# Two transposes of the first eight tiles, from the DMA queue to the matrix engine

## The chip, the core and the metric

The kernel runs on one core of a Trainium2 chip. The core has a matrix engine (TensorE, PE in the profile, with PEld for its weight loads), a vector engine (VectorE, DVE), a scalar engine (ScalarE, ACT), GpSimd (POOL) and SyncE (SP), which here issues DMAs alone. Data lies in SBUF, 128 partitions wide; matmuls write to PSUM, eight banks of 512 float32 per partition. The metric is the device time of one execution in microseconds (us); lower is better.

## What is computed

Eight batches of 576 rows, eight heads of 64. Keys and values are first averaged over groups of eight rows, so that each row of q meets 72 keys. Softmax, product with the averaged values, heads put side by side (512 columns), then a normalised row, a feed-forward block 512 to 2048 to 512, and the residual:

```python
    k_p = k.reshape(B, H, Sp, pool, D).mean(axis=3)
    v_p = v.reshape(B, H, Sp, pool, D).mean(axis=3)
    scores = scale * np.matmul(q, k_p.transpose(0, 1, 3, 2))
    scores = scores - np.max(scores, axis=-1, keepdims=True)
    attn = np.exp(scores)
    attn = attn / (np.sum(attn, axis=-1, keepdims=True) + 1e-09)
    return np.matmul(attn, v_p).astype(np.float32)
...
    xn = (x - mu) / np.sqrt(var + 1e-06) * g_ln
    ch = np.maximum(xn @ w_ch1, 0.0) @ w_ch2
    return (x + ch).astype(np.float32)
```

Inputs and output are float32. Nearly every product is made of float16 parts: a number x is split into hi = float16(x) and lo = float16(x - hi), and hi*hi + hi*lo + lo*hi are summed in PSUM.

## The kernel before

The 4608 rows are 36 tiles of 128 rows, t = 0 to 35; four tiles are a chunk, c = 0 to 8. Three stages work on a tile:

- **A.t** (`stage_a`: `scores`, `probs`). Four float32 matmuls (L279; each shows as two instructions in the profile) make the scores of 8 heads x 72 keys in PSUM. VectorE takes the row maximum (L288) and subtracts it into the SBUF tile `e` (L289). ScalarE makes the exponential (L298) and two float16 copies (L299, L302) into `phl`; GpSimd puts the low parts beside them (L306, L309); one DMA transpose on SP's queue (L316) brings the lot to `pt`, keys on partitions.
- **B.t** (`values`). Sixteen matmuls (L335, L336; 65 columns: 64 of v and one for the sum) multiply `pt` with the split values `va` and `vb`. VectorE and ScalarE normalise (L339 to L352), VectorE makes mean and variance (L356, L357) and the inverse root by three Newton steps of two one-column instructions each (L371, L374), and the normalised row `z` (L378). ScalarE makes its high part (L382), GpSimd the low part (L383), and a second DMA transpose (L387) writes both to `zT` of the chunk.
- **FFN.** `ffn_in` (L406) makes 128 rows of the hidden layer for up to 512 columns of `zT` in 12 matmuls; ScalarE and VectorE evict the high and low part (L414, L415). `ffn_out` (L435) multiplies back for one tile and one half of the hidden layer in 24 matmuls of 512 columns; VectorE adds the result to the residual (L445).

Beside the tiles the kernel prepares what they use: **C.m.b** converts a 1 MB block of weights that comes as 64-bit words into float32 (L163 and L175 on ScalarE, L166 and L167 on VectorE; 16 blocks), **S.m.b** splits one into hi (ScalarE, L138) and lo (VectorE, L139), once **M** has found the scale over half a matrix (a small matmul, L126, spreads a maximum over partitions). `load_k`, `pool_k`, `load_v`, `pool_v` load and average keys and values (**HK**, **HV** for half a batch; GpSimd, in batch 0 VectorE too), and `split_v` splits the values and copies them with four small DMAs to the second half of `va` and `vb`.

The order of recording is a table of tokens, `START`, for chunks 0 and 1 (A.0 to A.11, B.0 to B.11, all weights; **I.c.q** is a quarter of the hidden layer in `ffn_in`, in chunk 0 by half chunks, **O.c.h** a half of it in `ffn_out`), and a loop for chunks 2 to 8. The framework's scheduler then settles each engine's own order; engines run strictly in that order and wait for each other by semaphores. PSUM holds two banks for scores (`ps_s`), two for values (`ps_x`), and four single banks (`ps_f`).

Of the kernel before, what the change touches and what calls it, by code (L numbers as in the profile page):

```python
# [48 lines left out]
HK.1.1 R.2.1 S.1.0 HV.1.0 B.2 B.3 HV.1.1 A.4 S.1.1 S.1.2 A.5 S.1.3 C.2.1 I.0.0.0 R.1.4 B.4 C.1.4
I.0.1.0 B.5 R.2.2 A.6 R.2.3 B.6 I.0.1.1 C.2.3 A.7 C.2.2 C.2.0 M2.0 R.2.4 S.2.0 R.1.5 S.2.1 S.2.2  # L50
R.1.6 R.1.7 S.2.3 B.7 I.0.0.1 O.0.0 C.1.5 I.1.1 C.1.6 I.1.0 C.1.7 M1.1 S.1.4 S.1.5 O.1.0 R.2.5 S.1.6
R.2.6 S.1.7 C.2.4 I.0.2 A.8 R.2.7 C.2.5 C.2.7 HK.2.0 HV.2.0 C.2.6 HK.2.1 B.8 M2.1 S.2.4 A.9 HV.2.1
A.10 B.9 I.0.3 S.2.5 S.2.6 HK.3.0 HK.3.1 I.1.2 B.10 S.2.7 O.0.1 I.1.3 A.11 HV.3.0 B.11 HV.3.1 O.1.1
# [6 lines left out]
def attn_ffn_kernel(ctx: ExitStack, tc: tile.TileContext, qT, kT, v, g, w1, w2, out):  # L60
# [235 lines left out]
    def probs(t):  # L296
        e, ph = E.pop(t), phl[t % 2]
        nc.scalar.activation(out=e, in_=e, func=AF.Exp, scale=EXP_SCALE)  # L298
        nc.scalar.copy(  # L299
# [18 lines left out]
    def values(t):  # L318
# [11 lines left out]
        ps = ps_x.tile([P, 2, 512], F32, name="ps_x")  # L330
        px = ps[:, :, : H // 2 * (D + 1)].rearrange("p a (h d) -> p a h d", d=D + 1)
        for r, b in segs:
            for h in range(H):
# [1 line left out]
                nc.tensor.matmul(o, lhsT=pt[:, h, r], rhs=VA[b][:, h, :], start=True, stop=False)  # L335
# [46 lines left out]
        nc.scalar.copy(out=zhl[:, 0, :], in_=z)  # L382
        nc.gpsimd.tensor_tensor(out=zhl[:, 1, :], in0=z, in1=zhl[:, 0, :], op=ALU.subtract)  # L383
# [182 lines left out]
```

## Time and profile before

| | |
|---|---|
| runs | 903.48, 904.53, 905.30 us; median 904.53 |
| profiled execution | 902.32 us, of which 900.3 us from its first to its last instruction (the span) |
| busy in the span | PE 828.9, PEld 419.2, DVE 436.1, ACT 263.9, POOL 262.3 us |
| DMA traffic | 84.80 MB in 137288 packets |

The page cuts the span into 40 slices of 22.5 us and gives each engine's busy share in tenths. The rows of windows that follow give busy us (and instructions) of PE, PEld, DVE, ACT and POOL in a stretch, the granted clock of PE, the busy share of the 16 DMA engines and GB/s. Rows of a timeline give start, duration, engine, line, operation, tiles and shape, and in brackets the idle time before and what ended it. Rows of groups give busy us, mean ns of one, and the idle time in front of them.

### The profile page before, as it was taken

What the parts mean: (1) busy time and instruction counts of PE and PEld (TensorE: products, weight loads), DVE (VectorE), ACT (ScalarE), POOL (GpSimd) and SP (SyncE); (2) the same over time, 40 slices, a digit from 0 to 9 for tenths busy, and PEclk for the clock granted to TensorE, in tenths of its full rate; (3) what the DMA queues carried; (4) which work ended last, traced back from release to release, by engine and by line L of the source; (5) the groups of instructions that cost most, each with busy time, mean ns of one, the idle gap of its engine ahead of it and who ended that gap; (6) DMA issues with size and microseconds to landing.
All of it is one profiled execution on the core that took longest, in us unless ns stands there. A gap on an engine that the chain in (4) does not pass through costs nothing.

```text
span 900.3 us, 11947 instructions
## 1 busy us (share of the span) xinstructions
PE 828.9 (92%) x4524; PEld 419.2 (47%) x4524; DVE 436.1 (48%) x1022; ACT 263.9 (29%) x513; POOL 262.3 (29%) x414
## 2 busy tenths in 40 slices
PE   2247975999999999999999999999999999999998
PEld 2236733444444444454445544544544454444443
DVE  7797994335462543256335533653354335432121
ACT  3766743314131221223123312331232123211020
POOL 6796596104233150056002710230011002100000
PEclk9999996999999999999999999999999999999999
DMA  8999975102252313253223432332223121310001
GB/s 316 268 246 279 283 224 136 27 0 65 77 127 75 62 57 72 59 135 88 66 59 83 116 71 59 86 70 55 59 59 80 39 59 36 70 38 22 1 1 47
DMA packets 137288, 84.80 MB, mean 94 GB/s; under 512 B 116112, under 2 KB 117264, under 8 KB 135184
## 3 DMA queue, kind: packets, MB, share of 16 engines
q1 hardware_dynamic: 135696, 82.86, 35.2%
q10 hardware_dynamic: 1536, 1.20, 0.5%
q8 instruction: 35, 0.57, 0.3%
q14 instruction: 21, 0.17, 0.1%
HBM read 45.09 MB, written 9.44 MB: 61 GB/s over the span
## 4 chain that ended last, share of the span: by engine, by line
PE 84%; DMA 7%; DVE 5%; ACT 1%; issue 1%; SPq 1%; POOL 1%; ACTq 0%
PE ps_f L406 40%; PE ps_f L435 39%; PE ps_s L279 2%; DMA raw<-in_w_dram 2%; DMA vr<-in_v_dram 2%; PE ps_x L335 1%; DVE y L374 1%; PE ps_x L336 1%; DVE w L167 1%; DMA pt<-phl 1%; DMA ring<-in_w_dram 1%; DMA raw<-in_v_dram 1%; DMA zT<-hl 1%; DVE a L371 0%; DVE raw L166 0%
## 5 line engine op out<-in xcount | busy, mean ns | idle before, releaser
L406 PE MATMUL ps_f<-zT,w 128*128 128x512 f16 (+1 forms) x1824 | 385.2, 370 | 4.3 <-DVE ring L415 2.9
L435 PE MATMUL ps_f<-w,ring 128*128 128x512 f16 x1728 | 380.9, 380 | 6.2 <-DVE w L139 5.9
L406 PEld LDWEIGHTS <-w 128*128 128x128 f16 x1824 | 177.8, 98 | 194.4 <-issue 8.9
L435 PEld LDWEIGHTS <-ring 128*128 128x128 f16 x1728 | 168.6, 98 | 206.7 <-issue 8.5
L415 DVE SCALAR_TENSOR_TENSOR ring<-ps_f,ring 128x512 f16<-128x512 f32 (+1 forms) x152 | 99.6, 659 | 139.6 <-ACT ring L414 139.3
L414 ACT ACTIVATE ring<-ps_f 128x512 f16<-128x512 f32 (+1 forms) x152 | 86.9, 574 | 264.9 <-PE ps_f L406 240.8
L445 DVE SCALAR_TENSOR_TENSOR x<-ps_f,c_out,x 128x512 f32<-128x512 f32 x72 | 53.9, 748 | 190.6 <-PE ps_f L435 190.5
L306 POOL TENSOR_TENSOR phl<-e,phl 128x512 f16<-128x512 f32 x36 | 43.8, 1218 | 261.1 <-ACT phl L299 248.5
L279 PE MATMUL ps_s<-kblk,q 128*128 128x144 f32 (+1 forms) x320 | 56.3, 345 | 43.7 <-issue 23.2
L383 POOL TENSOR_TENSOR hl<-z,hl 128x512 f16<-128x512 f32 x36 | 42.1, 1169 | 126.1 <-ACT hl L382 122.1
L298 ACT ACTIVATE e<-e 128x576 f32<-128x576 f32 x36 | 24.6, 683 | 168.9 <-DVE e L289 162.9
L279 PEld LDWEIGHTS ps_s<-kblk,q 128*128 128x128 f32 (+1 forms) x320 | 49.0, 219 | 51.5 <-issue 33.8
L352 ACT ACTIVATE x<-ps_x,rs 128x64 f32<-128x64 f32 x144 | 33.3, 314 | 81.1 <-DVE x L345 46.0
L229 POOL TENSOR_TENSOR vr<-vr 72x256 f32<-72x256 f32 x56 | 44.8, 805 | 22.3 <-DMA vr<-in_v_dram 22.0
L299 ACT CAST phl<-e 128x1024 f16<-128x1024 f32 x36 | 37.5, 1042 | 5.3 <-DMA pt<-phl 4.8
L382 ACT CAST hl<-z 128x512 f16<-128x512 f32 x36 | 22.2, 618 | 55.0 <-DVE z L378 45.5
L356 DVE BATCH_NORM_STATS2 st<-x 128x6 f32<-128x512 f32 x36 | 24.9, 691 | 23.4 <-ACT x L352 23.3
L231 POOL TENSOR_TENSOR vp<-vr 72x64 f32<-72x64 f32 x56 | 18.5, 345 | 60.5 <-DVE vb L139 60.3
L219 POOL TENSOR_TENSOR kblk<-kr 64x72 f32<-64x72 f32 x58 | 23.8, 411 | 32.1 <-PE ps_s L279 29.2
L215 POOL TENSOR_TENSOR kr<-kr 128x288 f32<-128x288 f32 x29 | 24.1, 833 | 27.1 <-DMA kr<-in_kT_dram 26.8
L335 PE MATMUL ps_x<-va,pt 128*128 128x65 f16 (+1 forms) x320 | 27.4, 200 | 4.9 <-ACT x L352 3.5
L288 DVE TENSOR_REDUCE mx<-ps_s 128x8 f32<-128x576 f32 x36 | 27.0, 751 | 9.3 <-PE ps_s L279 9.2
(81 smaller groups left out, 488.8 us busy)
## 6 DMA issues: line engine op xcount, KB each, us to landing
raw<-in_w_dram SPq DMA_DIRECT2D x12, 1024.0 KB
q<-in_qT_dram SPq DMA_DIRECT2D x36, 256.0 KB
out_dram<-x SPq DMA_DIRECT2D x36, 256.0 KB
kr<-in_kT_dram SPq DMA_DIRECT2D x30, 288.0 KB
vr<-in_v_dram SPq DMA_DIRECT2D x56, 144.0 KB
ring<-in_w_dram SPq DMA_DIRECT2D x4, 1024.0 KB
raw<-in_v_dram SPq DMA_DIRECT2D x8, 144.0 KB
va<-vh ACTq DMA_DIRECT2D x16, 65.0 KB
```

What stands on the lines that cost most here:

```text
L229: eng.tensor_add(out=vr[:, 0:4, :], in0=vr[:, 0:4, :], in1=vr[:, 4:8, :])
L279: nc.tensor.matmul(ps[r, p // 2, p % 2 * 2 * KV : (p % 2 + 1) * 2 * KV], lhsT=q[:, p, r], rhs=kblk[b % NKB][:, p, :], start=True, stop=True,)
L299: nc.scalar.copy(out=ph[:, :, :, 0:KA], in_=e[:, :, 0:KA].unsqueeze(1).broadcast_to([P, 2, H, KA]))
L306: nc.gpsimd.tensor_tensor(out=ph[:, 0, :, KA:P], in0=e[:, :, 0:KA], in1=ph[:, 0, :, 0:KA], op=ALU.subtract)
L335: nc.tensor.matmul(o, lhsT=pt[:, h, r], rhs=VA[b][:, h, :], start=True, stop=False)
L352: nc.scalar.activation(out=xh[:, 4 + i, :], in_=px[:, 1, i, 0:D], func=AF.Copy, scale=rs[:, 4 + i : 5 + i])
L383: nc.gpsimd.tensor_tensor(out=zhl[:, 1, :], in0=z, in1=zhl[:, 0, :], op=ALU.subtract)
L406: nc.tensor.matmul(ps, lhsT=w[:, part, fs], rhs=zT[:, kz, cols], start=(n == 0), stop=(n == 3 * NKT - 1),)
L414: nc.scalar.activation(out=h[:, 0, i, cols], in_=ps, func=AF.Relu)
L415: nc.vector.scalar_tensor_tensor(out=h[:, 1, i, cols], in0=ps, scalar=0.0, in1=h[:, 0, i, cols], op0=ALU.max, op1=ALU.subtract,)
L435: nc.tensor.matmul(ps, lhsT=h[:, part, i, cols], rhs=w[:, wp, j], start=(n == 0), stop=(n == 3 * NFT // 2 - 1),)
L445: nc.vector.scalar_tensor_tensor(out=x, in0=ps, scalar=c_out[:, half : half + 1], in1=x, op0=ALU.mult, op1=ALU.add)
```

## The change

For tiles t < 8 (`XT`) both DMA transposes go. In `probs` the float32 `e` is transposed by eight matrix-engine transposes against a float32 identity (new line L306) into two PSUM banks, 72 partitions x 1024. ScalarE copies this to float16 as the high part (L311), VectorE subtracts that from PSUM for the low part (L312). In `values` such a tile takes 24 matmuls in place of 16 (hi with `vh`, hi with `vb`, lo with `vh`). In `ffn_in`'s input, `z` goes through four transposes (L409), a ScalarE copy (L410) and a VectorE subtraction (L411). The float16 copies, GpSimd subtractions and SP transposes of these tiles fall away; tiles 8 to 35 keep them. The four small DMAs of `split_v` fall away for batch 0. Scores, transposed probabilities and values share one PSUM pool `ps_2` of two two-bank buffers; the pool of small scalars has two buffers in place of three. `START` has the same tokens in another order.

```diff
--- before.py
+++ after.py
@@ -38,6 +38,7 @@
 NQ = 4
 FPQ = NFT // NQ
 NKB = 2
+XT = 8
 A_AT, B_AT = (0, 6, 10, 14), (5, 9, 13, 19)
 
 EXP_SCALE = 1.0 / (POOL * D**0.5)
@@ -45,12 +46,12 @@
 Z_EXP, W1_EXP = -2, 7
 OUT_EXP = -14 - Z_EXP - W1_EXP
 START = """
-LD K0 R.1.0 V0 A.0 R.1.1 B.0 A.1 R.1.2 C.1.2 C.1.0 B.1 A.2 R.1.3 C.1.1 HK.1.0 C.1.3 A.3 R.2.0 M1.0
...
+LD K0 V0 R.1.0 A.0 R.1.1 B.0 R.1.2 A.1 B.1 R.1.3 C.1.3 C.1.0 C.1.2 A.2 A.3 R.2.0 C.1.1 HK.1.0 HK.1.1
...
 """
 RSQRT_MAGIC = float(0x5F3759DF - 0x00400000)
 Z_VAR = 2.0 ** (-1 - 2 * Z_EXP)
@@ -67,9 +68,8 @@
     ring = ctx.enter_context(tc.tile_pool(name="ring", bufs=4))
     rawp = ctx.enter_context(tc.tile_pool(name="rawp", bufs=2))
     xres = ctx.enter_context(tc.tile_pool(name="xres", bufs=8))
-    small = ctx.enter_context(tc.tile_pool(name="small", bufs=3))
-    ps_s = ctx.enter_context(tc.tile_pool(name="ps_s", bufs=1, space=PSUM))
-    ps_x = ctx.enter_context(tc.tile_pool(name="ps_x", bufs=1, space=PSUM))
+    small = ctx.enter_context(tc.tile_pool(name="small", bufs=2))
+    ps_2 = ctx.enter_context(tc.tile_pool(name="ps_2", bufs=2, space=PSUM))
     ps_f = ctx.enter_context(tc.tile_pool(name="ps_f", bufs=4, space=PSUM))
 
 
@@ -82,6 +82,8 @@
     wm = {m: const.tile([P, WB], F32, name=f"wm{m}") for m in (1, 2)}
     ident = const.tile([P, P], BF16, name="ident")
     make_identity(nc, ident)
+    ident32 = const.tile([P, P], F32, name="ident32")
+    nc.scalar.copy(out=ident32, in_=ident)
     kblk = [const.tile([P, NPAIR, 2 * KV], F32, name=f"kblk{i}") for i in range(NKB)]
     phl = [const.tile([P, 2, H, P], F16, name=f"phl{i}") for i in range(2)]
     for t in kblk:
@@ -203,6 +205,7 @@
 
 
     kraw = {}
+    VH = {}
     VA, VB, CV, vp, vmax, vraw = {}, {}, {}, {}, {}, {}
 
     def load_k(b, p, kr=None, queue=nc.sync):
@@ -239,7 +242,8 @@
 
     def split_v(b):
         e, s = vmax.pop(b), scalar_tile("sv")
-        vh = wk1.tile([KV, H, D + 1], F16, name="vh")
+        VH[b] = vh = wk2.tile([KV, H, D + 1], F16, name="vh")
+        dup = (b + 1) * S > XT * P
         VA[b] = wk2.tile([P, H, D + 1], F16, name="va")
         VB[b] = wk2.tile([KB, H, D + 1], F16, name="vb")
         nc.vector.memset(vh[:, :, D : D + 1], 1.0)
@@ -248,7 +252,7 @@
         CV[b] = wk3.tile([P, 1], F32, name="cv")
         nc.vector.tensor_scalar_mul(out=CV[b], in0=e, scalar1=2.0**-16)
         split(vp.pop(b), s[:KV], vh[:, :, 0:D], VB[b][:KV, :, 0:D])
-        for i in range(2):
+        for i in range(2 if dup else 0):
             nc.scalar.dma_start(out=VA[b][i * KA : (i + 1) * KA], in_=vh[:KA])
             nc.scalar.dma_start(out=VB[b][KV + i * KR : KV + (i + 1) * KR], in_=vh[KA:])
 
@@ -273,7 +277,7 @@
         E[t] = e = wk1.tile([P, H, KV], F32, name="e")
         q = q_sb.pop(t)
         mx = scalar_tile("mx", H)
-        ps = ps_s.tile([P, 2, 512], F32, name="ps_s")
+        ps = ps_2.tile([P, 2, 512], F32, name="ps_2")
         for p in range(NPAIR):
             for r, b in segments(t):
                 nc.tensor.matmul(
@@ -296,6 +300,17 @@
     def probs(t):
         e, ph = E.pop(t), phl[t % 2]
         nc.scalar.activation(out=e, in_=e, func=AF.Exp, scale=EXP_SCALE)
+        if t < XT:
+            ps = ps_2.tile([P, 2, 512], F32, name="ps_2")
+            for h in range(H):
+                nc.tensor.transpose(
+                    out=ps[:KV, h // 4, h % 4 * P : (h % 4 + 1) * P], in_=e[:, h], identity=ident32
+                )
+            PT[t] = pt = wk2.tile([P, 2 * H, P], F16, name="pt")
+            hi, src = pt[:KV, 0:H], ps[:KV].rearrange("p a (h n) -> p (a h) n", n=P)
+            nc.scalar.copy(out=hi, in_=src)
+            nc.vector.tensor_tensor(out=pt[:KV, H:], in0=src, in1=hi, op=ALU.subtract)
+            return
         nc.scalar.copy(
             out=ph[:, :, :, 0:KA], in_=e[:, :, 0:KA].unsqueeze(1).broadcast_to([P, 2, H, KA])
         )
@@ -327,11 +342,17 @@
         pt = PT.pop(t)
         sm, rs = scalar_tile("sm", H), scalar_tile("rs", H)
         X[t] = x = xres.tile([P, DM], F32, name="x")
-        ps = ps_x.tile([P, 2, 512], F32, name="ps_x")
+        ps = ps_2.tile([P, 2, 512], F32, name="ps_2")
         px = ps[:, :, : H // 2 * (D + 1)].rearrange("p a (h d) -> p a h d", d=D + 1)
         for r, b in segs:
             for h in range(H):
                 o = px[r, h // 4, h % 4]
+                if t < XT:
+                    vl = VB[b][:KV, h, :]
+                    hi, lo = pt[:KV, h, r], pt[:KV, H + h, r]
+                    for n, (w, m) in enumerate(((hi, VH[b][:, h, :]), (hi, vl), (lo, VH[b][:, h, :]))):
+                        nc.tensor.matmul(o, lhsT=w, rhs=m, start=(n == 0), stop=(n == 2))
+                    continue
                 nc.tensor.matmul(o, lhsT=pt[:, h, r], rhs=VA[b][:, h, :], start=True, stop=False)
                 nc.tensor.matmul(
                     o, lhsT=pt[:KB, H + h, r], rhs=VB[b][:, h, :], start=False, stop=True
@@ -378,15 +399,21 @@
         nc.vector.tensor_scalar(
             out=z, in0=x, scalar1=mv[:, 0:1], scalar2=y, op0=ALU.subtract, op1=ALU.mult
         )
+        c, tt = divmod(t, TPC)
+        if tt == 0:
+            zTs[c] = wk2.tile([P, 2 * NKT, CH], F16, name="zT")
+        zT = zTs[c][:, :, tt * P : (tt + 1) * P]
+        if t < XT:
+            ps = ps_f.tile([P, CH], F32, name="ps_f").rearrange("p (k n) -> p k n", n=P)
+            for k in range(NKT):
+                nc.tensor.transpose(out=ps[:, k], in_=z[:, k * P : (k + 1) * P], identity=ident32)
+            nc.scalar.copy(out=zT[:, 0:NKT], in_=ps)
+            nc.vector.tensor_tensor(out=zT[:, NKT:], in0=ps, in1=zT[:, 0:NKT], op=ALU.subtract)
+            return
         zhl = wk2.tile([P, 2, DM], F16, name="hl")
         nc.scalar.copy(out=zhl[:, 0, :], in_=z)
         nc.gpsimd.tensor_tensor(out=zhl[:, 1, :], in0=z, in1=zhl[:, 0, :], op=ALU.subtract)
-        c, tt = divmod(t, TPC)
-        if tt == 0:
-            zTs[c] = wk2.tile([P, 2 * NKT, CH], F16, name="zT")
-        nc.sync.dma_start_transpose(
-            out=zTs[c][:, :, tt * P : (tt + 1) * P], in_=zhl.rearrange("p a d -> p (a d)")
-        )
+        nc.sync.dma_start_transpose(out=zT, in_=zhl.rearrange("p a d -> p (a d)"))
 
 
     hT = {}
```

What the scheduler makes of it is shown at three places. Line numbers of the changed kernel are up to 27 higher: L141 there is L139 before, L433 is L406, L442 is L415, L462 is L435, L472 is L445, L283 is L279, L292 and L293 are L288 and L289, L354 to L357 are the value matmuls.

**VectorE at the first split of a block of the second weight matrix (w2), which `O.0.0` needs.** Before, it stands among the work on tiles 5, 6 and 9 (`st` and `mv` are tile 5's, `sm` and `rs` tile 6's, `e` tile 9's):

```order
L356 BN_STATS st<-x 128x6
L289 TENSOR_TENSOR e<-ps_s,mx 128x576
L339 TENSOR_SCALAR sm<-ps_x 128x8
L167 SCALAR_TENSOR_TENSOR w_88<-w_88,raw 128x1024
L415 SCALAR_TENSOR_TENSOR ring<-ps_f,ring 128x256 x2
L357 BN_AGGR mv_878<-st 128x2
L342 RECIPROCAL rs<-sm 128x8
L139 SCALAR_TENSOR_TENSOR w_89<-w_89,ws 128x1024
```

Now it stands behind the sum, scale and normalisation of tile 7 (`sm`, `rs`, `x` are that tile's):

```order
L200 TENSOR_TENSOR ws<-f_88,s_1164 128x1
L360 TENSOR_SCALAR sm<-ps_1404 128x8
L249 MEMSET vh 72x8
L442 SCALAR_TENSOR_TENSOR ring<-ps_f,ring 128x256
L363 RECIPROCAL rs<-sm 128x8
L364 TENSOR_SCALAR rs<-rs,cv 128x8
L366 TENSOR_TENSOR x<-ps_1404,rs 128x256
L141 SCALAR_TENSOR_TENSOR w_86<-w_86,ws 128x1024
```

The rest of tiles 5 and 6 up to `z`, the sums of tile 7 and the last three of the 16 conversions have moved in front of the split; the scores of tiles 8 and 9 have moved behind it.

**The matrix engine where `O.0.0` begins (`ffn_out` of chunk 0, first half).** Before, the values of tile 6 follow its first matmul:

```order
L406 MATMUL ps_f<-zT,w_88 128x256
L435 LDWEIGHTS ring
L435 MATMUL ps_f<-w_89,ring 128x512
L335 LDWEIGHTS pt
L335 MATMUL ps_x<-va,pt 128x65
```

Now the values of tile 7 stand ahead of it, and three of the four score matmuls of tile 8 (`ps_1728`) follow its first matmul:

```order
L433 MATMUL ps_f<-zT,w_85 128x256
L462 LDWEIGHTS ring
L462 MATMUL ps_f<-w_86,ring 128x512
L283 MATMUL ps_1728<-kblk_102,q 128x144 x3
L462 LDWEIGHTS ring
```

Before, the values of tiles 6 and 7 and the scores of tile 10 lay among the matmuls of `O.0.0`; now those values stand ahead of it and those scores behind it.

**The matrix engine where `I.1.1` begins (first `ffn_in` of chunk 1, 512 columns).** Before, three of tile 11's score matmuls and those of tiles 12 and 13 stand in front of it, these with 64 rows for each of two batches (`kblk_102` and `kblk_103`):

```order
L279 MATMUL ps_s<-kblk_103,q 64x144
L279 MATMUL ps_s<-kblk_102,q 64x144
L279 MATMUL ps_s<-kblk_103,q 64x144
L406 LDWEIGHTS w_88
L406 MATMUL ps_f<-zT,w_88 128x512
```

Now `O.0.0` ends, then come the transposes of tile 7's `z`, the values of tile 8 and the scores of tile 9:

```order
L462 LDWEIGHTS ring
L462 MATMUL ps_f<-w_86,ring 128x512
L409 MATMUL ps_f<-ident_99,z 128x128 x4
L356 LDWEIGHTS pt
L356 MATMUL ps_1847<-va,pt 128x65
```

```order
L357 MATMUL ps_1847<-vb,pt 128x65
L283 MATMUL ps_1902<-kblk_101,q 128x144 x4
L433 LDWEIGHTS w_85
L433 MATMUL ps_f<-zT,w_85 128x512
```

In front of `I.1.1` there stood the scores of 14 tiles before, and now those of 10.

More of the change, by code (lines that the diff above doesn't have):

```diff
@@ L47 @@
 START = """
-LD K0 R.1.0 V0 A.0 R.1.1 B.0 A.1 R.1.2 C.1.2 C.1.0 B.1 A.2 R.1.3 C.1.1 HK.1.0 C.1.3 A.3 R.2.0 M1.0
[L49 to L53, printed above, removed]
+LD K0 V0 R.1.0 A.0 R.1.1 B.0 R.1.2 A.1 B.1 R.1.3 C.1.3 C.1.0 C.1.2 A.2 A.3 R.2.0 C.1.1 HK.1.0 HK.1.1
+HV.1.0 M1.0 R.2.1 S.1.0 B.2 S.1.1 B.3 HV.1.1 A.4 S.1.2 A.5 C.2.1 S.1.3 I.0.0.0 R.1.4 C.2.0 B.4 A.6
+R.2.2 I.0.1.0 B.5 I.0.1.1 C.2.2 B.6 R.2.3 C.2.3 C.1.4 M2.0 R.2.4 S.2.0 R.1.5 R.1.6 S.2.1 A.7 I.0.0.1
+C.1.6 R.1.7 S.2.2 S.2.3 C.1.5 O.0.0 HK.2.0 B.7 I.1.1 I.1.0 C.1.7 M1.1 S.1.4 O.1.0 R.2.5 S.1.5 S.1.6
+R.2.6 S.1.7 R.2.7 C.2.4 A.8 I.0.2 C.2.5 HK.2.1 C.2.6 HV.2.0 B.8 C.2.7 A.9 M2.1 S.2.4 S.2.5 HV.2.1
+A.10 S.2.6 I.0.3 B.9 HK.3.0 I.1.2 S.2.7 HK.3.1 A.11 B.10 I.1.3 B.11 O.1.1 HV.3.0 O.0.1 HV.3.1
 """
```

## The prediction

> I forecast a slower kernel: 914 us against the median of 904.53. What bounds the first 150 us stays where it is, on VectorE, and the new order puts 20 us of matmuls behind it that now run beside it.
>
> **What bounds the kernel now.** I read the slices first, then windows by stage, then the rows at the end of the first stage.
>
> ```profile
> span 900.3 us, 11947 instructions
> ...
> PE   2247975999999999999999999999999999999998
> ...
> DVE  7797994335462543256335533653354335432121
> ```
>
> PE is full from the seventh slice (about 150 us) on, and VectorE is full in front of that. The windows, cut at 40 us, at the end of tile 7's `z` (142.2) and at the first matmul of `I.1.1` (150.15):
>
> ```profile
> 0.00:20.00 20.00, 5.28 (x16) 3.92 (x16) 14.53 (x36) 4.73 (x6) 12.46 (x27) 1.00 0.88 302
> 0.00:40.00 40.00, 11.39 (x50) 8.91 (x50) 29.12 (x64) 18.62 (x26) 27.61 (x47) 1.00 0.99 309
> 40.00:142.20 102.20, 66.97 (x507) 48.58 (x508) 93.42 (x215) 64.37 (x123) 76.92 (x110) 0.97 0.92 244
> 0.00:142.20 142.20, 78.36 (x557) 57.49 (x558) 122.54 (x278) 83.00 (x148) 104.53 (x157) 0.98 0.94 262
> 150.15:900.30 750.15, 746.42 (x3944) 358.29 (x3943) 311.24 (x741) 176.97 (x359) 153.45 (x252) 1.00 0.25 62
> ```
>
> From 150.15 us PE is busy 746.4 of 750.15: whatever matmul stands there costs its full time. Before, VectorE works 122.5 of 142.2 us and idles 19.7: 10.9 in the first 40 us, where the DMA engines are full (0.99), and 8.8 in the next 102. So the span is the time at which `I.1.1` can start plus the matmuls left. What ends the first stage (timeline rows, and the fourth from the chain of waits):
>
> ```profile
> 141.67 0.53 DVE L378 TENSOR_SCALAR z<-x,mv,y 128x512 f32<-128x512 f32 x1
> 142.43 0.60 ACT L382 CAST hl<-z 128x512 f16<-128x512 f32 x1
> 143.16 1.15 POOL L383 TENSOR_TENSOR hl<-z,hl 128x512 f16<-128x512 f32 x1 [2.10 <-issue]
> 145.47 4.64 DMA zT<-hl
> 150.15 23.74 PE L406 MATMUL ps_f<-zT,w 128*128 128x512 f16 x96 [1.38 <-DMA zT<-hl]
> ```
>
> Tile 7's `z` leaves VectorE at 142.2; copy, subtraction and DMA transpose take 8 us more. By then `O.0.0` is long done: its first matmul ran at 103.61, its last group ended near 135, and in between it waited for VectorE's splits:
>
> ```profile
> 103.61 0.38 PE L435 MATMUL ps_f<-w,ring 128*128 128x512 f16 x1 [0.29 <-ACT w L138]
> 125.70 9.38 PE L435 MATMUL ps_f<-w,ring 128*128 128x512 f16 x36 [4.98 <-DVE w L139]
> ```
>
> **The change, part by part.** I count back from the end. Call S the moment at which VectorE ends the low part of tile 7's probabilities (the eighth L312). After S, PE's order in the changed kernel is fixed and nearly without gaps. The prices, from PE's timeline (the fifth from the chain of waits):
>
> ```profile
> 85.38 6.27 PE L406 MATMUL ps_f<-zT,w 128*128 128x256 f16 x56 [2.88 <-DVE ring L415]
> 97.08 0.19 PE L335 MATMUL ps_x<-va,pt 128*128 128x65 f16 x1
> 97.57 0.19 PE L336 MATMUL ps_x<-vb,pt 88*128 88x65 f16 x1
> 108.70 1.14 PE L279 MATMUL ps_s<-kblk,q 128*128 128x144 f32 x8
> 195.46 10.36 PE ps_f L406 x48
> 74.12 2.26 PE L279 MATMUL ps_s<-kblk,q 128*128 128x144 f32 x8 [2.25 <-DVE rowmax L104]
> ```
>
> (a) To the start of `O.0.0`: four groups of twelve 256-column matmuls (4 x 12 x 0.112 = 5.4), 24 value matmuls (0.49 us for 15 steps, so 0.8), tile 6's four transposes, a maximum and one score matmul (1.0), and two hand-overs through ScalarE and VectorE for PSUM buffers (1.6): 8.8 us. The first split's low part, 17 rows of VectorE's order behind S, is ready at about the same time. (b) `O.0.0`: 96 x 10.36/48 = 20.7; VectorE makes the other three splits while it runs. (c) Tile 7's transposes (0.4), values of tile 8 (0.5), scores of tile 8's last three pairs and of tile 9 (0.85 + 1.14): 2.9; the copy and subtraction of `z` end under these. (d) From `I.1.1` on: the old 750.15, plus the scores of tiles 10 to 13, which stood in front of it: 4 x 1.14 = 4.6. Sum: 8.8 + 20.7 + 2.9 + 754.8 = 787.2. So the span stays at 900.3 only if S comes by 113.1 us.
>
> VectorE's work up to S. From the groups of the first 150 us (the fourth row is one of 300 to 700 us):
>
> ```profile
> L288 DVE TENSOR_REDUCE mx<-ps_s 128x8 f32<-128x576 f32 x14 | 10.5, 750 | 5.4 <-PE ps_s L279 5.4
> L289 DVE TENSOR_TENSOR e<-ps_s,mx 128x576 f32<-128x576 f32 x13 | 9.7, 746 | 1.6 <-POOL phl L309 1.6
> L415 DVE SCALAR_TENSOR_TENSOR ring<-ps_f,ring 128x256 f16<-128x256 f32 x16 | 6.1, 415 | 4.2 <-ACT ring L414 4.2
> L415 DVE SCALAR_TENSOR_TENSOR ring<-ps_f,ring 128x512 f16<-128x512 f32 x72 | 49.5, 688 | 58.5 <-ACT ring L414 58.1
> L445 DVE SCALAR_TENSOR_TENSOR x<-ps_f,c_out,x 128x512 f32<-128x512 f32 x4 | 3.0, 738 | 0.0
> L139 DVE SCALAR_TENSOR_TENSOR w<-w,ws 128x1024 f16<-128x1024 f32 x4 | 5.9, 1481 | 0.0
> ```
>
> Up to tile 7's `z` the new order has three score pairs fewer (3 x 1.5 = 4.5), four residual additions fewer (3.0), and one tile's sum, inverse and scale fewer (some 0.7). It adds eight subtractions of 72x1024 and seven of 128x512 out of PSUM. No row shows the first; L415 reads the same kinds of operands and costs 415 ns for 256 columns and 688 for 512, so 1.2 us for 1024 (by L289's 746 for 576 it would be 1.3); the second is 0.69. That is 9.6 + 4.8. Work up to `z`: 122.5 - 8.2 + 14.4 = 128.7. Between S and `z` stand two L411 (1.4), eight evictions of 256 columns (3.3), four w2 splits (5.9), a score pair (1.5) and tile 7's normalisation (some 5): 17. So 111.7 up to S.
>
> From this comes off what GpSimd no longer does to VectorE:
>
> ```profile
> 119.90 4.42 DVE L374 SCALAR_TENSOR_TENSOR y<-a,y 128x1 f32<-128x1 f32 x1
> L374 DVE SCALAR_TENSOR_TENSOR y<-a,y 128x1 f32<-128x1 f32 x24 | 12.5, 522 | 0.2
> L374 DVE SCALAR_TENSOR_TENSOR y<-a,y 128x1 f32<-128x1 f32 x55 | 10.9, 198 | 1.7
> L371 DVE SCALAR_TENSOR_TENSOR a<-y,ve 128x1 f32<-128x1 f32 x24 | 8.4, 352 | 0.2
> L371 DVE SCALAR_TENSOR_TENSOR a<-y,ve 128x1 f32<-128x1 f32 x54 | 13.1, 242 | 1.7
> L306 POOL TENSOR_TENSOR phl<-e,phl 128x512 f16<-128x512 f32 x12 | 15.7, 1309 | 12.8 <-ACT phl L299 12.6
> L309 POOL TENSOR_TENSOR phl<-e,phl 128x64 f16<-128x64 f32 x12 | 5.1, 422 | 0.0
> L383 POOL TENSOR_TENSOR hl<-z,hl 128x512 f16<-128x512 f32 x8 | 9.7, 1214 | 8.4 <-ACT hl L382 6.2 <-issue 2.1
> ```
>
> A one-column instruction of 0.2 us took 4.42 while GpSimd ran one operation after the other. In the first stage the two Newton lines are 24 x (522 - 198) + 24 x (352 - 242) = 10.4 us longer than later. Of GpSimd's 104.5 us the lines that go are 30.5 (29%; the part of tiles 8 to 11 moves behind S). The relief lies between 29% of 10.4, 3.0, and the whole 10.4; since the longest stretches come from GpSimd operations in a row, I take 6.4, above the share: 105.3 us of work.
>
> Idle time up to S. The first 40 us I leave at 10.9: their loads of keys, values and weights stay, and one tile at a time now goes VectorE, ScalarE, PE, ScalarE, VectorE. The DMA transposes there cost no more than SP's queue; the least is the 5.5 of the first 20 us. Behind 40 us the rate of before (8.8 in 102.2) gives 6.6 over some 76 us. DMA relief is not counted here: weights come earlier, but VectorE's list is no shorter. S = 105.3 + 10.9 + 6.6 = 122.8, and the span 122.8 + 787.2 = 910.0, 9.7 more than before. The profiled execution took 902.32 with a span of 900.3; the median of the runs is 4.2 above that span. On the median the forecast is 904.5 + 9.7 = 914.
>
> **The transposes** themselves, 96 of them, I count on PE's idle time: in 40 to 142 us PE idles 35 us. Their price is bounded by a value matmul's step (97.08 to 97.57: 33 ns for 65 columns, so 65 ns for 128) and by a float32 score matmul at its slow rate (2.26 us for four of 144 columns, so 0.50 us for 128): 6 to 48 us. I take 0.11, near the float16 end, as each is one instruction in the order and a score matmul is two in the trace. Removed at no gain, as their engines wait anyway: ScalarE's two copies against its new one, and 16 SP transposes. The four small DMAs and the pools I cost at nothing; two shared two-bank buffers hold PE back only where VectorE is late with a subtraction, which the idle time above holds.
>
> [...]
>
> **Rivals.** *VectorE comes free* (faster). All 10.4 us of stretch go, idle time behind 40 us vanishes, and the emptier DMA queue cuts the first 40 us to 5.5 idle: S = 101.3 + 5.5 = 106.8, 6.3 before the break-even point: 898. For it speaks the DMA share of 0.99; against it that S then allows no wait at all. *PE becomes the bound* (slower still). Transposes at 0.50 us: the 36 of tiles 4 to 7 that lie among `I.0` (24 for probabilities, 12 for `z`) cost 14 us more where PE has 16 groups of 1.34 us to do as well, and VectorE waits for both: 928. It decides from about 0.3 us each. *No change*: the two errors cancel, S near 113: 904.5.
>
> **How the numbers follow.** Forecast 0.50, PE bound 0.17, VectorE free 0.25, no change 0.08. The range goes from 897, under the faster rival, to 930, above the slower one. Around the likeliest alone it is 907 to 921 (relief 3 to 10.4, idle 4 us either way). 0.2%, 1.8 us, is about what a measurement here can tell from nothing. Faster 0.24, same 0.09, slower 0.67.
>
> **What would show it.** Right: `O.0.0` starts near 132 us and runs without gaps to `I.1.1` near 155; 755 us follow; VectorE is 85% busy up to S; L374 falls towards 200 ns. Wrong: VectorE idles less than 8 us up to S; or L306 shows 0.3 us or more; or `O.0.0` starts before 122.

## The result, and the profile after

| | before | after |
|---|---|---|
| median of four runs, us | 904.91 | 913.39 |
| lowest to highest | 903.48 to 905.56 | 913.01 to 913.53 |
| span of the profiled execution | 900.3 | 911.2 |
| first matmul of `O.0.0` | 103.6 | 133.4 |
| first matmul of `I.1.1` | 150.2 | 156.9 |
| from there to the end | 750.2 | 754.3 |

The ratio is 1.0087, with a 95% interval of 1.0068 to 1.0105: the change makes the kernel 0.9% slower. The forecast was 914.0.

The page of the changed kernel, span and slices of 22.8 us:

```profile
span 911.2 us, 12223 instructions
...
PE   2433799999999999999999999999999999999998
...
DVE  7978784336273555246424552553254335432121
...
PEclk9965799999999999999999999999999999999999
```

PE is full from the sixth slice on (114 us), where before it was full from 150, and the span is longer all the same: what fills it early is the work of the first stage, now closer together. The granted clock falls in the slices three to five. How much of that is new, and what the row says of the first slices, is taken up in the last section.

The windows of the changed kernel, cut at S (123.38, the end of the eighth L312) and at the first matmul of `O.0.0` (PE, PEld, VectorE, ScalarE, GpSimd busy, granted clock, DMA share, GB/s):

```profile
0.00:123.38 123.38, 60.45 (x470) 50.77 (x471) 103.36 (x245) 68.16 (x115) 69.44 (x116) 0.79 0.66 227
0.00:40.00 40.00, 14.69 (x89) 11.36 (x89) 32.93 (x73) 18.35 (x27) 24.63 (x45) 1.00 0.85 296
40.00:123.38 83.38, 45.76 (x381) 39.41 (x382) 70.43 (x173) 49.81 (x88) 44.82 (x72) 0.69 0.57 194
123.38:133.40 10.02, 10.02 (x111) 9.11 (x109) 7.22 (x22) 5.58 (x13) 0.67 (x2) 1.00 0.11 29
```

VectorE works 103.4 of the 123.4 us up to S. From S to `O.0.0` PE has no gap, but S is not where the gaps end. The last one in front of `O.0.0` ends at 111.25 us, 12 us before S:

```profile
111.25 2.29 PE L283 MATMUL ps<-kblk,q 128*128 128x144 f32 x8 [0.75 <-ACT x L373]
113.00:133.40 20.40, 20.40 (x195) 18.38 (x193) 17.31 (x55) 10.86 (x26) 3.22 (x7) 0.94 0.13 35
```

VectorE's groups of the first 140 us of the changed kernel (busy us, mean ns of one, idle time in front of it and what ended it):

```profile
L312 DVE TENSOR_TENSOR pt<-ps,pt 72x1024 f16<-72x1024 f32 x8 | 9.7, 1218 | 0.5 <-ACT pt L311 0.5
L168 DVE TENSOR_SCALAR raw<-raw 128x1024 int32<-128x1024 int32 x12 | 9.2, 770 | 7.9 <-DMA raw<-in_w_dram 7.9
L392 DVE SCALAR_TENSOR_TENSOR a<-y,ve 128x1 f32<-128x1 f32 x24 | 6.4, 279 | 0.1
L395 DVE SCALAR_TENSOR_TENSOR y<-a,y 128x1 f32<-128x1 f32 x23 | 5.0, 222 | 0.1
L411 DVE TENSOR_TENSOR zT<-ps_f,zT 128x512 f16<-128x512 f32 x7 | 4.8, 681 | 0.0
```

L392 and L395 are the Newton lines (352 and 522 ns before). New is the wait of 7.9 us for weights in front of L168 (0.5 us in front of L166 before). The timeline of the changed kernel, with two groups of transposes and the end of the first stage:

```profile
79.44 1.92 PE L306 MATMUL ps<-ident,e 128*72 128x128 f32 x8 [3.95 <-ACT e L302]
104.04 1.07 PE L306 MATMUL ps<-ident,e 128*72 128x128 f32 x8 [2.11 <-ACT e L302]
122.16 1.22 DVE L312 TENSOR_TENSOR pt<-ps,pt 72x1024 f16<-72x1024 f32 x1
130.86 1.27 DVE L141 SCALAR_TENSOR_TENSOR w<-w,ws 128x1024 f16<-128x1024 f32 x1
133.40 0.38 PE L462 MATMUL ps_f<-w,ring 128*128 128x512 f16 x1
134.35 20.67 PE L462 MATMUL ps_f<-w,ring 128*128 128x512 f16 x95
154.85 0.60 PE L409 MATMUL ps_f<-ident,z 128*128 128x128 f32 x4
156.87 0.81 PE L433 MATMUL ps_f<-zT,w 128*128 128x512 f16 x3
```

`O.0.0` runs as one block, and `I.1.1` follows it at once. The first split that `O.0.0` needs (L141) ends at 132.1, 1.3 us before it starts: there PE is behind with its own matmuls, and VectorE is not what it waits for.

### The profile page after: what moved, and what is told of

The parts are those of the page before. It is cut to its first block, busy times and chain, and to the rows that moved or that the text cites. A ratio compares the mean times of both kernels' runs of the same rounds, so it can differ in the third digit from the quotient of the medians.

```text
span 911.2 us, 12223 instructions
## 1 busy us (share of the span) xinstructions
PE 841.9 (92%) x4692; PEld 433.7 (48%) x4692; DVE 442.5 (49%) x1038; ACT 262.7 (29%) x506; POOL 237.6 (26%) x390
## 4 chain that ended last, share of the span: by engine, by line
PE 81%; DMA 7%; POOL 5%; DVE 4%; issue 1%; ACT 1%; SPq 0%; POOLq 0%; DVEq 0%; ACTq 0%
PE ps_f L433 38%; PE ps_f L462 37%; DMA kr<-in_kT_dram 3%; PE ps L283 3%; POOL vr L232 2%; DMA raw<-in_w_dram 1%; DMA pt<-phl 1%; POOL kr L218 1%; DMA vr<-in_v_dram 1%; PE ps L356 1%; POOL vr L233 1%; PE ps L357 1%; POOL vp L234 1%; DMA raw<-in_v_dram 1%; DVE w L169 1%
## 5 line engine op out<-in xcount | busy, mean ns | idle before, releaser
L433 PE MATMUL ps_f<-zT,w 128*128 128x512 f16 (+1 forms) x1824 | 384.0, 369 | 0.0
L462 PE MATMUL ps_f<-w,ring 128*128 128x512 f16 x1728 | 378.9, 379 | 0.6 <-DVE ring L442 0.6
L433 PEld LDWEIGHTS <-w 128*128 128x128 f16 x1824 | 177.6, 98 | 187.5 <-issue 0.4
L462 PEld LDWEIGHTS <-ring 128*128 128x128 f16 x1728 | 168.3, 98 | 200.3 <-DVE ring L442 1.1
L442 DVE SCALAR_TENSOR_TENSOR ring<-ps_f,ring 128x512 f16<-128x512 f32 (+1 forms) x152 | 99.8, 659 | 142.6 <-ACT ring L441 139.1
L472 DVE SCALAR_TENSOR_TENSOR x<-ps_f,c_out,x 128x512 f32<-128x512 f32 x72 | 53.9, 748 | 196.8 <-PE ps_f L462 192.4
L321 POOL TENSOR_TENSOR phl<-e,phl 128x512 f16<-128x512 f32 x28 | 32.8, 1170 | 252.1 <-ACT phl L314 237.4
L283 PE MATMUL ps<-kblk,q 128*128 128x144 f32 (+1 forms) x320 | 50.4, 322 | 20.3 <-ACT x L373 9.3
L415 POOL TENSOR_TENSOR hl<-z,hl 128x512 f16<-128x512 f32 x28 | 32.4, 1157 | 115.0 <-ACT hl L414 113.2
L373 ACT ACTIVATE x<-ps,rs 128x64 f32<-128x64 f32 x144 | 33.3, 315 | 100.2 <-DVE x L366 66.5
L283 PEld LDWEIGHTS ps<-kblk,q 128*128 128x128 f32 (+1 forms) x320 | 45.0, 203 | 28.9 <-ACT x L373 9.6
L218 POOL TENSOR_TENSOR kr<-kr 128x288 f32<-128x288 f32 x29 | 27.9, 966 | 43.2 <-DMA kr<-in_kT_dram 42.8
L414 ACT CAST hl<-z 128x512 f16<-128x512 f32 x28 | 17.3, 618 | 50.7 <-DVE z L399 47.2
L399 DVE TENSOR_SCALAR z<-x,mv,y 128x512 f32<-128x512 f32 x36 | 30.0, 834 | 2.8 <-DVE y L395 0.5
L292 DVE TENSOR_REDUCE mx<-ps 128x8 f32<-128x576 f32 x36 | 27.0, 750 | 5.0 <-PE ps L283 4.9
L314 ACT CAST phl<-e 128x1024 f16<-128x1024 f32 x28 | 29.2, 1042 | 0.5
```

Of the source, the lines that this page charges most:

```text
L218: eng.tensor_add(out=kr[:, 0:4, :], in0=kr[:, 0:4, :], in1=kr[:, 4:8, :])
L283: nc.tensor.matmul(ps[r, p // 2, p % 2 * 2 * KV : (p % 2 + 1) * 2 * KV], lhsT=q[:, p, r], rhs=kblk[b % NKB][:, p, :], start=True, stop=True,)
L321: nc.gpsimd.tensor_tensor(out=ph[:, 0, :, KA:P], in0=e[:, :, 0:KA], in1=ph[:, 0, :, 0:KA], op=ALU.subtract)
L373: nc.scalar.activation(out=xh[:, 4 + i, :], in_=px[:, 1, i, 0:D], func=AF.Copy, scale=rs[:, 4 + i : 5 + i])
L399: nc.vector.tensor_scalar(out=z, in0=x, scalar1=mv[:, 0:1], scalar2=y, op0=ALU.subtract, op1=ALU.mult)
L433: nc.tensor.matmul(ps, lhsT=w[:, part, fs], rhs=zT[:, kz, cols], start=(n == 0), stop=(n == 3 * NKT - 1),)
```

## The experiments

Differences "to the change" are against its median of 913.39; the kernel before had medians of 904.6 to 905.6 beside every group of runs.

### The two halves of the change alone

The new operations with the old order, and the old operations with the new order:

```diff
 START = """
-LD K0 V0 R.1.0 A.0 R.1.1 B.0 R.1.2 A.1 B.1 R.1.3 C.1.3 C.1.0 C.1.2 A.2 A.3 R.2.0 C.1.1 HK.1.0 HK.1.1
...
+LD K0 R.1.0 V0 A.0 R.1.1 B.0 A.1 R.1.2 C.1.2 C.1.0 B.1 A.2 R.1.3 C.1.1 HK.1.0 C.1.3 A.3 R.2.0 M1.0
...
```

> The changed kernel with the token order of before: transposes on the matrix engine alone, without the new order. My theory (VectorE's longer list, then O.0.0 behind it, sets the start of I.1.1): nearly the same price as the change itself, since the subtractions L312 and L411 stay on VectorE; VectorE's work up to the split that lets O.0.0 run goes up and O.0.0 starts between 125 and 135 us; median 910 to 915. Rival, the new order is what costs time: 905, within 2 us of before. Rival, the new order was a repair of the transposes: slower than the change, above 916.

> Before with the token order of the change: DMA transposes kept, the order alone. My theory: without the subtractions VectorE reaches the first split of w2 earlier and the score groups of 17 tiles stand in front of I.1.1, so the order alone costs little: 902 to 908. Rival, the order alone (O.0.0 behind VectorE's list) makes the loss: 912 to 916.

Measured: the transposes alone 931.67 (ratio to before 1.0296, 1.0269 to 1.0323), the order alone 912.10 (1.0085, 1.0054 to 1.0115). So 27 us and 7 us, and together only 8.5. The operations' half holds the shared PSUM pool and the smaller pool of scalars too, and in each half the scheduler made every engine's order anew; what each of these is worth in the 27 us was not measured. My theory's number is wrong in both; the transposes alone are the third case named there, the order a repair of what the new operations cost. For the order alone the rival's number came, but not for its reason, as the timeline of that kernel shows:

```profile
113.76 4.70 PE L435 MATMUL ps_f<-w,ring 128*128 128x512 f16 x21
...
151.04 0.54 DVE L378 TENSOR_SCALAR z<-x,mv,y 128x512 f32<-128x512 f32 x1
153.69 1.15 POOL L383 TENSOR_TENSOR hl<-z,hl 128x512 f16<-128x512 f32 x1
...
159.16 2.06 PE L406 MATMUL ps_f<-zT,w 128*128 128x512 f16 x5
```

`O.0.0` starts at 113.8, 20 us before the change's. But tile 7's `z` comes at 151.0 in place of 141.7, and the same 8 us of copy, subtraction and DMA transpose follow it.

In the other kernel `O.0.0` starts at 144.1 and `I.1.1` at 165.1, 8.2 us after the change's. It has 763.6 us behind that, against 754.3: 7.1 of them in one wait of PE for a `zT` at 302.6 us.

### Less work, more time: the order moves when a price moves

Two edits meant to test the bound: L312 left out (its lines follow; the low part of the probabilities is then missing from the result), and every transpose done twice.

```diff
-            nc.vector.tensor_tensor(out=pt[:KV, H:], in0=src, in1=hi, op=ALU.subtract)
...
-                    for n, (w, m) in enumerate(((hi, VH[b][:, h, :]), (hi, vl), (lo, VH[b][:, h, :]))):
+                    for n, (w, m) in enumerate(((hi, VH[b][:, h, :]), (hi, vl))):
```

> The change without the eight subtractions L312 and without the 64 value matmuls that read their result: the low part of the probabilities of tiles 0 to 7 is left out of the computation. It takes 8 x 1.22 = 9.7 us from VectorE and some 2 us from the matrix engine. My theory (VectorE's list bounds the stage): O.0.0 starts 5 to 10 us earlier and the time falls by 5 to 10 us, to 903 to 908. Rival, waits for weights or the chain of one tile bound it, and VectorE only waits longer elsewhere: less than 3 us, 911 or more.

> The change with each of its 96 matrix-engine transposes done twice, the second over the first. My theory: only the 24 transposes after about 113 us, where the matrix engine has no gap, cost their full 0.107 us, 2.6 us in all; the others fill gaps: 2 to 6 us over the change, 915 to 919. Rival, the matrix engine bounds the stage: 96 x 0.107 to 96 x 0.21, so 10 to 20 us over the change, 924 to 934.

Measured: 928.93 without L312 (15.5 us *more* than the change) and 927.18 with doubled transposes (13.8 more). The first is against both theories. The timeline of the kernel without L312 shows why:

```profile
165.07 0.67 DVE L398 TENSOR_SCALAR z<-x,mv,y 128x512 f32<-128x512 f32 x1
165.80 1.11 PE L408 MATMUL ps_f<-ident,z 128*128 128x128 f32 x4 [8.16 <-DVE z L398]
167.56 0.69 DVE L410 TENSOR_TENSOR zT<-ps_f,zT 128x512 f16<-128x512 f32 x1 [1.82 <-ACT zT L409]
```

With other prices the scheduler puts tile 7's `z` behind the four residual additions of `O.0.0`, to 165.1 (the change: 140.3), and PE waits 8.2 us for it. So neither run says anything on the bound. From here on I wrote every engine's order down (the list of its instructions, each tied to the one before it) and changed that list or the operations by hand. The list alone, without an edit, was not timed. Behind `I.1.1` the first kernel that holds it took 754.1 us against the change's 754.3, so no cost of the list shows there.

### The same two edits with the order held

```diff
+def pin(tc):
+    have = {i.name: i for i in tc.nc.cur_bb.bb.instructions}
+    for order in PIN.values():
...
+            tc.add_manual_dep(
+                have[b], a, mybir.DependencyInfo(mybir.DependencyClass.NoSync, mybir.DependencyReason.DATA),
...
-            nc.vector.tensor_tensor(out=pt[:KV, H:], in0=src, in1=hi, op=ALU.subtract)
+            nc.vector.tensor_tensor(out=pt[:KV, H:, 0:1], in0=src[:, :, 0:1], in1=hi[:, :, 0:1], op=ALU.subtract)
```

> The changed kernel with every engine's order written down as the change has it, and the eight subtractions L312 cut from 72x1024 to 72x8; the value matmul that would read the low part reads the high part once more, so the low part of the probabilities of tiles 0 to 7 is left out of the computation, at the same number of instructions. VectorE loses 8 x 1.1 = 8.6 us and nothing changes its place, unlike in the run that left L312 out. Theory (VectorE's list bounds the stage up to O.0.0): 4 to 8.6 us under the change, 905 to 909, part of the saving going into waits for weights before 100 us. Rival (weights or the chain of one tile bound it): less than 2 us, above 911.

> The changed kernel with every engine's order written down as the change has it, and each of the 96 transposes done twice in a row. Theory: the 24 behind 113 us cost 0.107 us each, 2.6 us in all, those in front fill gaps of the matrix engine: 2 to 5 us over the change, 915 to 919; then most of the 13.8 us of the run that doubled them without a fixed order was its other order. Rival, the matrix engine or the chain through it bounds the stage: 10 us or more, above 923.

Measured: 908.63 with the short L312 (1.0042 of before, 1.0027 to 1.0057), 4.8 us under the change, within what my theory allowed and far from the rival's 2. VectorE's group, PE's last wait and the window of that kernel up to its `O.0.0`:

```profile
L312 DVE TENSOR_TENSOR pt<-ps,pt 72x8 f16<-72x8 f32 x8 | 1.5, 186 | 1.1 <-ACT pt L311 1.1
...
107.13 2.29 PE L283 MATMUL ps<-kblk,q 128*128 128x144 f32 x8 [1.05 <-ACT x L373]
...
0.00:129.37 129.37, 69.21 (x579) 59.15 (x580) 104.39 (x266) 73.76 (x128) 65.55 (x118) 0.75 0.64 219
```

The eight subtractions cost 8.3 us less; VectorE's work up to `O.0.0` falls from 110.58 (of 133.40) to 104.39 (of 129.37), its idle time rises from 22.8 to 25.0, and `O.0.0` comes 4.0 earlier. About half of what is taken from VectorE reaches the end. PE's last wait ends 4.1 us earlier (107.13 for 111.25), and from there to `O.0.0` PE takes 22.2 us without a gap in both kernels: a shorter list of VectorE pays through that wait alone. VectorE is the first bound up to it, not the only one.

Doubled transposes with the order held: 919.59 (1.0155, 1.0134 to 1.0176), 6.2 us over the change. That lies between my 2 to 5 and the rival's 10, so more than half of the unheld run's 13.8 was its order, and a second set of 96 transposes costs 6.2 us. They don't fill gaps for nothing. A tile's transposes, PE's last wait and `O.0.0`:

```profile
83.42 3.46 PE L307 MATMUL ps<-ident,e 128*72 128x128 f32 x16 [4.30 <-ACT e L302]
...
115.30 2.29 PE L283 MATMUL ps<-kblk,q 128*128 128x144 f32 x8 [1.30 <-DVE a L393]
...
140.23 0.38 PE L464 MATMUL ps_f<-w,ring 128*128 128x512 f16 x1
```

A tile's eight transposes stand between its exponential and its copy, so 1.5 us more of them at 83 us make that tile later, while PE still waits 4.3 us in front of them. Of the 6.8 us by which `O.0.0` is late (140.23 for 133.40), 4.1 stand in front of PE's last wait, which ends at 115.30. The other 2.8 lie in the stretch without gaps, where my theory had 2.6.

### GpSimd's work given back

```diff
+            for cut in (slice(0, 512), slice(512, 576)):
+                gp(ph, cut)
...
+        nc.gpsimd.tensor_tensor(out=lo, in0=some, in1=hi, op=ALU.subtract)
```

> The changed kernel with its order written down and, on GpSimd alone, 24 more operations on constants of the sizes and at the places of the subtractions that the change took from it (8 of 128x512 and 8 of 128x64 behind the exponentials, 8 of 128x512 behind z); nothing waits for them. My sum took 6.4 us off VectorE's work for what GpSimd no longer does to it (bounds 3.0 to 10.4). If that holds, the Newton lines go back from 222 and 279 ns towards 522 and 352, VectorE's work up to the splits rises by 3 to 10 us and the time by 3 to 9, to 916 to 922. Rival, the two engines do not disturb each other and the lines were longer for another reason: within 2 us of the change, 911 to 915.

Measured: 925.36 (1.0235, 1.0213 to 1.0256), 12.0 us over the change; the rival of no disturbance is out, and the effect is above my upper bound. VectorE's Newton lines and the window up to `O.0.0` in that kernel:

```profile
L402 DVE SCALAR_TENSOR_TENSOR a<-y,ve 128x1 f32<-128x1 f32 x24 | 17.0, 722 | 0.1
...
L405 DVE SCALAR_TENSOR_TENSOR y<-a,y 128x1 f32<-128x1 f32 x23 | 5.5, 243 | 0.1
...
0.00:146.74 146.74, 72.99 (x578) 60.86 (x579) 122.62 (x266) 73.93 (x128) 95.02 (x141) 0.79 0.57 193
```

No order on VectorE differs from the change's, and one Newton line goes from 279 to 722 ns, 10.6 us in 24 instructions; the other hardly moves (222 to 243). VectorE's work up to `O.0.0` is 122.6 us for 110.6, the same list 12.0 us longer, its idle time 24.1 for 22.8, and `O.0.0` starts at 146.7 for 133.4. GpSimd is busy 95.0 us up to there, for 70.1.

### Seven weight conversions moved behind the splits

In both kernels all or most of the 16 conversions stand in VectorE's order ahead of the splits that `O.0.0` needs, though it needs only four blocks of the second matrix. Only places in the written order change here; each conversion is L168 and L169 (L166, L167 before), two ScalarE lines and a load.

The first two of them, as VectorE's order shows them:

```diff
-L168 TENSOR_SCALAR raw<-raw 128x1024
-L169 SCALAR_TENSOR_TENSOR w_86<-w_86,raw 128x1024
...
 L141 SCALAR_TENSOR_TENSOR w_86<-w_86,ws 128x1024
 L392 SCALAR_TENSOR_TENSOR a<-y,ve 128x1
+L168 TENSOR_SCALAR raw<-raw 128x1024
 L395 SCALAR_TENSOR_TENSOR y<-a,y 128x1
 L399 TENSOR_SCALAR z<-x,mv_1438,y 128x512
-L472 SCALAR_TENSOR_TENSOR x<-ps_f,c_out,x 128x512 x4
+L169 SCALAR_TENSOR_TENSOR w_86<-w_86,raw 128x1024
+L168 TENSOR_SCALAR raw<-raw 128x1024
+L169 SCALAR_TENSOR_TENSOR w_85<-w_85,raw 128x1024
```

> The changed kernel with its order written down, but with the last seven of the 16 weight conversions (blocks 2.4 and later in the order of loading; none is needed by O.0.0) moved on VectorE, ScalarE and the load queue behind the four splits of w2, among the work on O.0.0 and I.1.1. VectorE's list up to the splits is shorter by 7 x (0.66 + 1.14) = 12.6 us and by 1 to 4 us of waits for weights. Theory (VectorE's list up to the splits sets when O.0.0 and I.1.1 start): 9 to 16 us under the change, 897 to 904. Rival, another chain (evictions, the tiles' own) takes over: 908 or more. Rival, the late conversions hold up the second half of the hidden layer: the start of I.1.1 is earlier but the time behind it grows by as much.

> The kernel before with its order written down and the same seven conversions moved behind tile 7's z. VectorE's list up to that z is shorter by 12.6 us. Theory (VectorE's list up to z of tile 7 sets the start of I.1.1 in the kernel before): I.1.1 8 to 13 us earlier than 150, 892 to 897. Rival, GpSimd and the transposes of the DMA queue or the matrix engine's own work take over: 900 or more.

On the changed kernel: 905.26, no difference from before (0.9991, 0.9971 to 1.0012), 8.1 us under the change. `O.0.0` starts at 122.4, 11.0 us earlier, with 99.2 us of VectorE's work in front of it for 110.6. `I.1.1` gains only 8.3 of it in the profiled execution. The timeline says where the rest went (L409 are tile 7's transposes, L410 ScalarE's copy of them):

```profile
143.85 0.60 PE L409 MATMUL ps_f<-ident,z 128*128 128x128 f32 x4
146.92 1.17 ACT L165 ACTIVATE w<-raw 128x1024 f32<-128x1024 f32 x1 [2.56 <-DMA raw<-in_w_dram]
147.97 0.59 ACT L410 CAST zT<-ps_f 128x512 f16<-128x512 f32 x1
148.61 1.01 PE L433 MATMUL ps_f<-zT,w 128*128 128x512 f16 x2 [2.58 <-ACT zT L410]
```

The copy is queued behind a late conversion that waits for its weights, which I had put there. The time behind `I.1.1` is 757.8, 3.4 longer: my third case, in part. This execution took 908.15 us, 2.9 above the median of the ten: 8.3 less 3.4 is 4.9, and the medians differ by 8.1. So most of the ten lost less than these rows show; where, is not known.

On the kernel before: 898.79 (0.9926, 0.9901 to 0.9951), 6.1 us faster than before, a little above my range. `z` of tile 7 comes at 134.45 in place of 141.67 and `I.1.1` at 143.06, 7.1 us earlier, where I had expected 8 to 13:

```profile
134.45 0.53 DVE L378 TENSOR_SCALAR z<-x,mv,y 128x512 f32<-128x512 f32 x1
135.21 0.60 ACT L382 CAST hl<-z 128x512 f16<-128x512 f32 x1
136.24 1.70 POOL L383 TENSOR_TENSOR hl<-z,hl 128x512 f16<-128x512 f32 x1 [2.39 <-issue]
138.25 1.24 SPq L387 DMA_TRANSPOSE zT<-hl  x1
143.06 1.46 PE L406 MATMUL ps_f<-zT,w 128*128 128x512 f16 x3 [0.21 <-DMA zT<-hl]
```

The tail of 8.6 us from `z` is what is left, and there a matrix-engine transpose belongs.

### One transpose of the change, where it pays

```diff
+        if t == 7:
+            ps = ps_f.tile([P, CH], F32, name="ps_f").rearrange("p (k n) -> p k n", n=P)
+            for k in range(NKT):
+                nc.tensor.transpose(out=ps[:, k], in_=z[:, k * P : (k + 1) * P], identity=ident32)
+            nc.scalar.copy(out=zT[:, 0:NKT], in_=ps)
+            nc.vector.tensor_tensor(out=zT[:, NKT:], in0=ps, in1=zT[:, 0:NKT], op=ALU.subtract)
+            return
```

> The kernel before with the late conversions as in the run before, and in addition z of tile 7 alone transposed by the matrix engine in place of ScalarE's copy, GpSimd's subtraction and the DMA transpose, and the scores of tile 13 behind the first 24 matmuls of I.1.1. The way from z of tile 7 to I.1.1 was 8.5 us before (141.67 to 150.15) and 8.6 there; four transposes at 0.11 to 0.21, a copy near 0.9 and a subtraction of 0.69 make 2.0 to 2.6. Theory: I.1.1 starts 5 to 7 us earlier than 143.1, 891 to 895. Rival, the chain of scores and exponentials of tiles 12 and 13 on VectorE, ScalarE and GpSimd holds up the evictions: 897 to 901.

> As the run before (z of tile 7 alone by the matrix engine, seven conversions late), with three things mended that its trace showed: the four transposes stand ahead of the scores of tile 12, the first two evictions of I.1.1 stand ahead of the subtraction of tile 13's maximum, and the conversions from the third on stand later, where their weights have landed (the matrix engine had waited 12 us for evictions behind its start of I.1.1 at 139.2, and ScalarE 6.5 us for weights). Theory: I.1.1 near 138 and at most 756 us behind it, so 893 to 898. Rival, what waits for the late blocks (the second half of the hidden layer) takes it back: 899 to 906.

The first attempt: 906.04 (1.0006, 0.9985 to 1.0026), the rival. `I.1.1` starts at 139.2, 3.9 earlier than in the run before, but 764.6 us follow it. PE's and ScalarE's rows of that kernel:

```profile
166.76 1.12 ACT L165 ACTIVATE w<-raw 128x1024 f32<-128x1024 f32 x1 [6.50 <-DMA raw<-in_w_dram]
...
169.14 3.15 PE L414 MATMUL ps_f<-zT,w 128*128 128x512 f16 x7 [6.69 <-DVE ring L423]
```

A conversion placed before its weights had landed held ScalarE for 6.5 us, and with it the evictions, and with them PE. This is the longest of several waits of PE there. The second attempt places the transposes, two evictions and the conversions by these rows: 889.47 (0.9827, 0.9792 to 0.9862), 1.7% faster than the kernel before, 24 us faster than the change, and below my 893.

```profile
135.35 0.53 DVE L380 TENSOR_SCALAR z<-x,mv,y 128x512 f32<-128x512 f32 x1
...
135.94 1.12 PE L390 MATMUL ps_f<-ident,z 128*128 128x128 f32 x4 [5.50 <-DVE z L380]
137.09 0.58 ACT L391 CAST zT<-ps_f 128x512 f16<-128x512 f32 x1 [0.89 <-PE ps_f L390]
137.71 0.69 DVE L392 TENSOR_TENSOR zT<-ps_f,zT 128x512 f16<-128x512 f32 x1 [1.83 <-ACT zT L391]
138.77 2.71 PE L414 MATMUL ps_f<-zT,w 128*128 128x512 f16 x6
```

From the end of `z` (135.9) to `I.1.1` it is now 2.9 us in place of 8, and from there PE never waits: 749.7 us to the end. Against the kernel with the late conversions alone, `I.1.1` starts 4.3 us earlier, as the way from `z` to it is shorter, and 3.4 us less follow it, with evictions and conversions in new places. So not all of the gain is the transposes'.

## Why the prediction was right, point by point

**Counting back from S** held to a microsecond in the sum, with its terms off by up to one. (a) 10.0 us for 8.8; (b) 21.6 for 20.7; (c) 1.9 for 2.9; (d) 754.3 for 754.8; together 787.8 for 787.2. The three score pairs of tile 8, counted in (c), ran inside `O.0.0`, which moves some 0.7 us from (c) to (b). Term (a) was right in size and wrong in content: it had 48 matmuls of 256 columns and 1.6 us of hand-overs, where PE ran 77 of them without a hand-over.

That S is what releases `O.0.0` did not hold. PE was full from 111.25 us on, 12 us before S, and what it had still to do set the start of `O.0.0`. From any moment of such a stretch the time to the end can be counted back; that S fell into it, and at the forecast moment, was in part luck.

**S** came at 123.4 for 122.8, but by errors that offset each other. VectorE's work was 103.4 for 105.3, its idle time 20.0 for 17.5. (The prediction's first reading is loose as well: the seventh slice of the kernel before stands at 5, as the 150 us at which PE fills lie inside it.)

- The prices of the new subtractions, taken from L415, were right: 1218 for 1200 ns, 681 for 690.
- *The relief from GpSimd* was taken too small. The Newton lines alone fell by 23 x 300 + 24 x 73 ns = 8.7 us where the term had 6.4. By the sum the whole relief was 8.3 us (111.7 less 103.4). The run that gives GpSimd as many operations back shows that the effect is real and of that order, 12.0 us of VectorE's work; it is not the term itself, as those operations wait for nothing and hit the other Newton line.
- *Idle time* was nearly right in sum and wrong in both parts. In the first 40 us it was 7.1 for 10.9 (40.00 less 32.93). Behind 40 us it was 13.0 for 6.6, and 7.9 us of that are waits for weights at L168. Weights did come earlier: the last load was issued at 92.8 us, at 118.5 before. But the conversions had moved ahead by more (the last L169 starts at 103.6 us, the last L167 before at 133.6). SyncE's waits up to 125 us show what holds the loads (L156): the conversions that still hold the two buffers, and loads of values that wait for GpSimd and stand in the same queue (us in total, times, longest):

```profile
SPq L226 <- POOL vp L234: 26.4, 9, 6.1
SPq L156 <- ACT raw L177: 23.4, 8, 5.2
```

- *The transposes counted on PE's idle time* is the step that failed. Their price of 0.11 us was right at 104 us (1.07 / 8 = 0.13; from one start to the next 0.109) and half of the true one earlier (1.92 / 8 = 0.24; 0.213). By the trace 68 of the 96 ran at the slower step, so together they took some 17.5 us of PE (68 x 0.213 + 28 x 0.109) where the prediction had 10.6. And they aren't free where PE waits: a second set costs 6.2 us in the order held. What the first set costs was not measured by itself; if it is near that, the forecast owes its accuracy to a relief that was larger by about as much.

From its start to its end one transpose of the changed kernel takes 0.27 us where the clock on record is 1.00 (at 104 us), and 0.42 where it is 0.50 (at 79 us). In a row one starts every 0.109 or 0.213 us, and eight end after 1.07 or 1.92 us: the step, and not the time of one, is what PE pays.

**What bounds the stage.** Up to 111 us VectorE's list in the main, shown by the short L312 (half of 8.3 us comes through) and by the late conversions (11.0 of 12.6 us at `O.0.0`); waits for weights and the chain of one tile through PE and ScalarE take the rest. From 111 us to `O.0.0` it is PE, whose first 4 us there run at half the clock (0.50 up to 115.4). VectorE was busy 84% of the time up to S (forecast 85).

**The rivals.** *VectorE comes free* fell: L395 went to 222 ns, but idle time grew behind 40 us. *PE becomes the bound*, at 0.3 us per transpose, was not reached at 0.24, and its 928 fell. Its mechanism held in part: PE has no gap in the last 22 us before `O.0.0`, and there each transpose costs its step. *No change* fell. That the operations cost 27 us in the old token order, the prediction did not see, as it read the two only together.

## What to carry to other kernels

Where a scheduler sets the order from prices, an experiment that changes a price also changes the order, and can move the time further and the other way than the edit: write the order down before the edit is timed. Work that a later stage needs should not stand in front of the work that the matrix engine waits for, on the engine that is busiest there. A transpose on the matrix engine pays at the one place where the matrix engine waits for its result (2.9 us for 8 here), and costs where the engine that evicts it is the bound (here 4.8 us come back when the eight L312 are cut short).
